# Routing operations handed out four at a time late in the attention, and the first second-layer weights' differences moved from VectorE to GpSimd

## The chip, the cores and the metric

The kernel runs on one core of a Trainium2 chip. The metric is the device time of one execution in microseconds. Three runs of the kernel before gave 551.42, 549.42 and 554.98 us, with a median of 551.42 us.

## What is computed

A block attention feeds a mixture of experts. The attention has 4 batches, 8 heads, 768 positions and head size 64. Each query sees a window of its neighbours (distance under 16) and 24 block summaries (maximum of the keys and mean of the values over 32 positions). Its output, 3072 tokens of 512 numbers, goes through a two-level router:

```
g_idx = argmax(x @ w_group);  e_idx = argmax(x @ w_expert[g_idx])
h = relu(x @ w1[g, e]);  out = (g_w * e_w) * (h @ w2[g, e])
```

There are 4 groups of 4 experts, so 16 experts, each with a 512x1024 and a 1024x512 matrix. One token goes to one expert. Everything is float32; the expert products are made from a rounded part and the difference to it (three matmuls for one product).

## The kernel before

**Attention.** `attention` (L591) runs 48 steps and three more that drain the pipeline (L905). A step scores a third of a head pair (`scores`), takes exponentials on ScalarE (`exps`), transposes them on TensorE and copies them out on ScalarE (`transpose_p`), multiplies by the values (`values`, whose results VectorE divides by the row sums into `xt`), and works on the next head pair (`prep`: copies `kf` and `kw`, block maxima `ks`) and on the router's logits (`logits`: transposes of `xt`, the copy `xT`, and the matmul into `ps_lg`). Each engine takes its work in the order in which it is written; the order is made by hand, and no scheduler changes it.

**Routing inside the attention.** For three of the four batches the router's work is handed out in between. `Router.route` and `Router.ranks` turn logits into expert, rank inside the expert and weight, some 27 small VectorE operations a batch (maxima `mx`, differences `dd`, one-hots `c` and `eoh`, casts `sb` and `eb`, then seven small ranking matmuls on TensorE, then `rk`, `sums`, `rf`, `ri`, the one-hot rows `ohr`, and the weights `we`, `wf`, `w_all`). They are generators that stop after each operation, and they are added to a list after steps 16, 28 and 40. The second one is followed by `first_blocks`, which finds the largest expert and makes the tables `t_first_gather`, `t_first_weight` and `t_first_scatter` of its first four blocks of 128 tokens. `advance` (L597) takes operations off the list: one behind `scores`, one behind the reciprocal of `values`, one behind its multiplication, two in `prep` part 4 (`OPS`, L61). It stops early at a pause. In the attention `clock.pe` is minus infinity, so a pause before a matmul always lasts until the next step. What is left when the steps are over is written out in one piece (L962).

**The hook.** Late steps also start the experts (`hook`, L1350): the difference of the first expert's first weights is made in four parts behind steps 44 to 47 (`split_w`: ScalarE rounds `w1h`, VectorE subtracts to `w1l`), the tokens are gathered by GpSimd behind steps 44 and 47, and the first blocks of matmuls of `first` are written behind steps 49 to 51.

**First expert blocks.** `first` (L1261) handles two pairs of 128-token blocks. `stage1_2` makes the hidden layer in eight groups of 12 matmuls (k = 0 to 7), with a rounding `hTh` on ScalarE and a difference `hTl` on VectorE after every second group; `stage2` makes the outputs, 24 matmuls a block. In the first pair, groups k = 4 to 7 each write one quarter of the second weights' rounding `w2h` on ScalarE and of their difference `w2l` on VectorE (L1264).

**Routing behind the attention.** The fourth batch's routing, the tables of all units (`units`, `unit_rows`, `unit_slots`) and their matmuls `ps_lg<-bo_unit` form one generator, `fin`. The main loop (L1403) hands its operations out after each group of matmuls by the planner's own count: `clock.pe` grows by an estimate for each matmul (107 for a 256-column one, 213 for a 512-column one), `clock.dve` by 85 plus the columns for each VectorE instruction, and operations are handed out while `clock.dve` is below `clock.pe`. A pause waits until `clock.pe` is 300 (ranking) or 800 (table matmuls) ahead. What is left when `first` reports "units" is written in one piece. Then the pairs of all experts follow (`pair`, L1147).

Of the kernel before, what the change touches and what calls it, by code (L numbers as in the profile page):

```python
# [58 lines left out]

ROUTE_AT = (16, 28, 40)  # L60
OPS = dict(r=1, m=1, k=2, s=(1, 1, 1))  # L61


W1_AT = 34
# [10 lines left out]
class Banks:  # L75
# [5 lines left out]
    def next(self):  # L81
        self.n += 1
        return self.tiles[(self.n - 1) % len(self.tiles)]
# [6 lines left out]
class Clock:  # L90

    pe, dve = float("-inf"), 0.0
    step = 0


def columns(ap):
# [494 lines left out]
def attention(tc, q, k, v, w_group, w_expert, ident, x_dram, ps, router, hook):  # L591
# [3 lines left out]
    clock = router.clock  # L595

    def advance(ops):  # L597

        for _ in range(ops):
            r = next(work[0], work) if work else "wait"  # L600
            if r is work:
                work.pop(0)
            elif r == "wait":
                break

    def need(bit):

        while not router.ready & bit:
            clock.step += 1
            advance(99)  # L610
# [5 lines left out]
    with ExitStack() as st, ExitStack() as nat_st:  # L616
# [54 lines left out]
        def init_va(i):  # L671
            va = va_ring[i]
            V.memset(va[0:PAD, 0], 0.0)
            V.memset(va[64:KW, NQT - 1], 0.0)

            nc.gpsimd.memset(va[96:NR, :, :, 0:D], 0.0)
            V.memset(va[96:NR, :, :, D:D + 1], EPS)
            V.memset(va[0:NC, :, :, D:D + 1], 1.0)
# [40 lines left out]
        def block_sums(idx):  # L719

            sp = ps_tr.next()[:, 0:2 * D]
            va = va_ring[idx % NVA]
            for i in range(NQT // 4):
                for j in range(4):
                    T.matmul(out=sp[32 * j:32 * j + 32], lhsT=pick[:, i], rhs=va[0:KW, NQT // 4 * j + i, :, 0:D],
                             start=(i == 0), stop=(i == NQT // 4 - 1), skip_group_check=True)
            vss[idx] = sm.tile([P, 2 * D], F32, name="vs", bufs=2)
            V.tensor_copy(out=vss[idx], in_=sp)
# [8 lines left out]
        def put_vs(idx):  # L737
            vs = vss.pop(idx)
            vr = wk.tile([NC, 1, 2, D], F32, name="vr")
            n = NBLK // 4  # L740
            for j in range(4):
                nc.sync.dma_start(out=vr[KW + n * j:KW + n * j + n, 0].rearrange("p h d -> p (h d)"), in_=vs[32 * j:32 * j + n])
            vrs[idx] = vr
# [10 lines left out]
        def copy_1port(out, src):  # L754

            V.tensor_reduce(out=out, in_=src.unsqueeze(src.ndim), axis=AX.X, op=ALU.max)

        def prep(idx, part):
# [27 lines left out]
            else:  # L786
# [5 lines left out]
                             in_=kf[:, PAD:PAD + S].rearrange("p (a k) -> p a k", k=BLOCK))  # L792
                advance(OPS["k"])
                copy_1port(kw[:, :, KW:NC], ks[:, None, :].broadcast_to([P, NQT, NBLK]))

        def scores(n):

            idx, g = n // 3, n % 3
            qt, kw = qts[idx % 2], kws[idx % 2]
            sp = [ps_s.next()[:, 0:2 * NC].rearrange("p (j c) -> p j c", j=2) for _ in range(2)]  # L800
            for j in range(2):
                for i, h in ((0, 0), (1, 1), (1, 0), (0, 1)):
                    t, rows = 4 * g + 2 * j + i, slice(64 * h, 64 * h + 64)
                    T.matmul(out=sp[h][64 * i:64 * i + 64, j], lhsT=qt[rows, QT * t:QT * t + QT],
                             rhs=kw[rows, t], start=True, stop=True, skip_group_check=True)
            nm = sm.tile([P, 4], F32, name="nm")
            ss = sm.tile([P, 4, NC], F32, name="ss", bufs=2)
            for h in range(2):
                for j in range(2):
                    u, t = 2 * h + j, 4 * g + 2 * j  # L810
                    V.tensor_tensor_reduce(out=ss[:, u], in0=mask[:, 1 if t == 0 else 2 if t == NQT - 2 else 0],  # L811
                                           in1=sp[h][:, j], scale=1.0, scalar=3.4e38, op0=ALU.add, op1=ALU.min,
                                           accum_out=nm[:, u:u + 1])
            advance(OPS["s"][g])
            return ss, nm

        def exps(n, sp, nm):
            pr = prr[n % 3]
            for i in range(4):
                nc.scalar.activation(out=pr[:, i, 0:NC], in_=sp[:, i], func=AF.Exp, bias=nm[:, i:i + 1], scale=-1.0)  # L820
            return pr

        def transpose_p(pr):
            pt = ps_tr.next()
            for i in range(4):
                T.transpose(out=pt[0:NR, i * P:(i + 1) * P], in_=pr[:, i], identity=ident)
            ptS = wk.tile([NR, 4, P], F32, name="ptS", bufs=3)
            nc.scalar.copy(out=ptS.rearrange("p a c -> p (a c)"), in_=pt[0:NR])  # L828
            return ptS

        def values(idx, g, ptS):
# [3 lines left out]
            for u in range(4):  # L835
                h, j = u // 2, u % 2
                for i in range(2):
# [4 lines left out]
            V.reciprocal(out=rs, in_=av[:, :, :, D:D + 1])  # L842
            advance(OPS["r"])
            V.tensor_tensor(out=x[:, 2 * g:2 * g + 2, 2 * a * D:2 * (a + 1) * D].rearrange("p j (h d) -> p j h d", h=2),
                            in0=av[:, :, :, 0:D], in1=rs.broadcast_to([P, 2, 2, D]), op=ALU.mult)
            advance(OPS["m"])

# [57 lines left out]

        for n in range(NG + 3):
            idx, g = n // 3, n % 3
            if n < NG:
                b, a = order[idx]
                xs[b] = x_ring[b % 2]  # L910
            for step in PLAN[g]:
                if step == "s" and n < NG:
                    sps = scores(n)
                    if n == 0:
                        block_sums(0)
                        put_vs(0)
                        router.consts()
                elif step == "e" and n < NG:
                    prs[n] = exps(n, *sps)
                elif step == "t" and 0 <= n - T_LAG < NG:  # L920
                    pts[n - T_LAG] = transpose_p(prs.pop(n - T_LAG))
                elif step == "v" and 0 <= n - V_LAG < NG:
                    values((n - V_LAG) // 3, (n - V_LAG) % 3, pts.pop(n - V_LAG))
                elif step[0] == "p" and n < NG and idx + 1 < len(order):
                    prep(idx + 1, int(step[1]))
                elif step == "b" and n < NG and idx + 1 < len(order):
                    block_sums(idx + 1)
                elif step[0] == "l" and 0 <= idx - LAG[step] < len(order):
                    logits(idx - LAG[step], int(step[1]))
            if n == 0:  # L930
                init_va(2)
                spread_vs(0)
                init_va(3)
            if n in ROUTE_AT:
                b1 = ROUTE_AT.index(n)
                work.append(router.route(b1 * TB, (b1 + 1) * TB))
                if b1 == 1:
                    work.append(router.first_blocks())
            if n == NG - 4:
                nat_st.close()  # L940
            if n < NG:
                if g == 0 and 0 < idx < len(order) - 3:
                    qk[idx + 3] = load_qk(idx + 3)
                if g == 0 and idx + 2 < len(order):
                    load_vw(idx + 2)
                if g == 2 and idx + 1 < len(order):
                    put_vs(idx + 1)
                if g == 0 and idx > 0:
                    spread_vs(idx)
            if g == 1 and stores:  # L950
                store()
            while stores and n == NG - 5:
                store()
            clock.step += 1
            hook(n, need, w1_space)
# [11 lines left out]
class Experts:  # L967
# [293 lines left out]
    def first(self):  # L1261
        for i in range(0, NE, 2):
            for k, _ in enumerate(self.stage1_2(0)):
                if i == 0 and k >= 4:  # L1264
                    self.split_w(("first", 0), 1, [k - 4])
                yield
            if i + 2 < NE:
                self.x_t1()
                yield
            for half in range(2):  # L1270
                s2 = self.stage2([t[:, :, half * P:half * P + P] for t in self.hT2], ("first", i + half))
                if i + half < NE - 1:
                    yield from s2
        yield "units"
        for part, _ in enumerate(s2):
            self.split_w(("unit", 0), 0, [part])
            if part == 0:
                self.x_t2(0)
                for i in range(2):
                    self.gather_one(i)  # L1280
                self.gather_small(0)
        self.fixed = True
# [153 lines left out]
```

## Time and profile before

| | before |
|---|---|
| median of three runs | 551.42 us |
| the profiled execution | 553.0 us |
| its span | 551.3 us |
| mean granted TensorE clock | 0.953 of 2.4 GHz |
| TensorE busy | 496.8 us (90%) |
| VectorE busy | 312.7 us (57%) |
| ScalarE busy | 288.9 us (52%) |
| GpSimd busy | 152.9 us (28%) |

The span runs from the first to the last instruction; the execution's own time is 1.7 us longer. The attention lasts until about 200 us of the span, the first expert's blocks until about 258 us, and the other units follow. In rows of a timeline the first number is the start and the second the length in us; in brackets stands the idle time of the engine just before and what ended it. PE is TensorE, DVE VectorE, ACT ScalarE, POOL GpSimd, SPq the queue of SyncE's transfers. L122 is the helper that records every operation of the router and the experts, so those rows are told apart by their tiles.

### The profile page before, as it was taken

To read this page: it belongs to the slowest core of one execution; us is meant where nothing else is said; L and a number is where in the kernel's file an instruction comes from. 1 tells how busy PE (TensorE), PEld (TensorE's weight loads), DVE (VectorE), ACT (ScalarE), POOL (GpSimd) and SP (SyncE) were. 2 spreads that over 40 slices of the span, in tenths; PEclk is the share of its full clock that TensorE was granted. 3 is DMA by queue.
4 is the path that set the end of the run, shared out by engine and by line. 5 is a ranking of instruction groups with operands and counts; after the bars stand their busy time and mean duration, and the time that the engine had idled before them with its cause. 6 is when DMAs were issued, how large, how long until landed. Compare 5 with 4: busy or idle time off the path is not lost. (4 is left out here: it accounts for less than half of the span.)

```text
span 551.3 us, 13196 instructions
## 1 busy us (share of the span) xinstructions
PE 496.8 (90%) x4873; PEld 416.4 (76%) x4873; DVE 312.7 (57%) x1001; ACT 288.9 (52%) x561; POOL 152.9 (28%) x166
## 2 busy tenths in 40 slices
PE   7798888898988688989979999999999999999990
PEld 4576666676767577978959798889898998977760
DVE  6767778788866558866715445365474745630000
ACT  4788867899967433215615444455463644631110
POOL 6553533353444100045122040402021230211110
PEclk8899979999988799997999999999999999999996
DMA  9676855795671610099918969667656667637930
GB/s 212 148 186 152 204 143 140 165 213 146 142 269 40 248 59 21 19 352 394 365 37 314 356 251 393 235 211 272 214 203 224 210 213 248 212 121 251 340 117 27
DMA packets 80840, 111.18 MB, mean 202 GB/s; under 512 B 42732, under 2 KB 51310, under 8 KB 77936
## 3 DMA queue, kind: packets, MB, share of 16 engines
q1 hardware_dynamic: 74992, 93.31, 54.3%
q0 software_dynamic: 4704, 14.69, 7.1%
q10 hardware_dynamic: 1056, 2.10, 1.1%
q8 instruction: 45, 0.74, 0.6%
q14 instruction: 43, 0.35, 0.2%
HBM read 122.46 MB, written 13.04 MB: 246 GB/s over the span
## 5 line engine op out<-in xcount | busy, mean ns | idle before, releaser
L122 PE MATMUL ps_s<-xT,w1h 128*128 128x256 f32 x448 | 85.1, 287 | 1.9 <-DVE hTl L122 1.5
L122 DVE TENSOR_TENSOR w2l<-w2r,w2h 128x1024 fp32r<-128x1024 f32 x40 | 48.8, 1225 | 54.4 <-ACT w2h L1061 52.6
L1105 POOL DMA_INDIRECT out_dram<-y,t_unit_scatter x21 | 23.8, 1134 | 197.4 <-ACT y L1099 112.7
L122 PEld LDWEIGHTS ps_s<-xT,w1h 128*128 128x128 f32 x448 | 71.5, 193 | 3.4 <-DVE hTl L122 1.7
L122 PE MATMUL ps_s<-xT,w1l 128*128 128x256 f32 x224 | 63.7, 285 | 0.0
L820 ACT ACTIVATE pr<-ss,nm 128x120 f32<-128x120 f32 x192 | 60.1, 388 | 3.6 <-DVE nm L811 3.2
L1143 ACT ACTIVATE hTh<-ps_s 128x512 fp32r<-128x512 f32 x44 | 26.3, 598 | 54.1 <-PE ps_s L122 34.1
L749 POOL TENSOR_TENSOR va<-vr,share 24x512 f32<-24x512 f32 x48 | 49.7, 1060 | 11.7 <-DMA vr<-vs 8.3
L122 DVE TENSOR_TENSOR w1l<-w1r,w1h 128x1024 fp32r<-128x1024 f32 x40 | 46.4, 1221 | 2.9 <-ACT w1h L1061 2.9
L122 PE MATMUL ps_s<-ohr,w1h 128*128 128x256 f32 x256 | 48.1, 286 | 0.0
L122 DVE SCALAR_TENSOR_TENSOR hTl<-ps_s,hTh 128x512 fp32r<-128x512 f32 x44 | 30.4, 691 | 25.6 <-ACT hTh L1143 25.4
L811 DVE CUSTOM_DVE_ANT_0 ss<-mask,ps_s 128x120 f32<-128x120 f32 x192 | 42.0, 273 | 4.1 <-ACT pr L820 2.5
L1061 ACT CAST w2h<-w2r 128x1024 fp32r<-128x1024 f32 x40 | 41.5, 1042 | 4.3 <-DVE w_all L122 3.6
L122 PEld LDWEIGHTS ps_s<-xT,w1l 128*128 128x128 f32 x224 | 43.2, 193 | 0.2
L122 PEld LDWEIGHTS ps_s<-ohr,w1h 128*128 128x128 f32 x256 | 40.5, 192 | 0.7 <-issue 0.6
L828 ACT COPY ptS<-ps_tr 121x512 f32<-121x512 f32 x48 | 28.1, 586 | 21.8 <-PE ps_tr L122 8.7
L1061 ACT CAST w1h<-w1r 128x1024 fp32r<-128x1024 f32 x40 | 38.9, 1047 | 0.0
L789 POOL COPY kw<-kf 128x1152 f32<-128x1152 f32 x15 | 17.4, 1157 | 77.3 <-DVE kf L780 43.3
L122 PE MATMUL ps_s<-kw,qt 64*64 64x120 f32 x768 | 34.4, 290 | 4.4 <-DVE nm L811 2.3
L776 ACT ACTIVATE qt<-ps_tr 64x384 f32<-64x384 f32 x64 | 33.4, 522 | 5.9 <-PE ps_tr L122 4.9
L122 PE MATMUL ps_s<-ohr,w1l 128*128 128x256 f32 x128 | 36.3, 284 | 0.0
L122 PE MATMUL ps_av<-va,ptS 121*64 121x65 f32 x768 | 34.3, 234 | 2.0 <-DVE mx L122 1.3
(255 smaller groups left out, 1058.5 us busy)
## 6 DMA issues: line engine op xcount, KB each, us to landing
w1r<-in_moe_w_dram SPq DMA_DIRECT2D x42, 1024.0 KB
w2r<-in_moe_w_dram SPq DMA_DIRECT2D x42, 1024.0 KB
va<-in_v_dram SPq DMA_DIRECT2D x32, 240.0 KB
kn<-in_k_dram SPq DMA_DIRECT2D x16, 384.0 KB
qn<-in_q_dram SPq DMA_DIRECT2D x16, 384.0 KB
x_dram<-xt SPq DMA_DIRECT2D x12, 512.0 KB
w_first<-in_moe_w_dram SPq DMA_DIRECT2D x2, 1024.0 KB
w2r<-in_moe_w_dram ACTq DMA_DIRECT2D x2, 1024.0 KB
```

Of the source, the lines that this page charges most:

```text
L122: return f(*args, **kw)
L749: nc.gpsimd.tensor_tensor(out=va_ring[idx % NVA][KW:NC, t:t + n, :, 0:D], in0=vr[KW:NC].broadcast_to([NBLK, n, 2, D]), in1=by(share, KW, N ...
L776: nc.scalar.activation(out=by_run(qb, h)[:, j], in_=tv, func=AF.Copy, scale=-1.0 / 8.0)
L789: (nc.gpsimd if idx else V).tensor_copy(out=kw[:, :, 0:KW], in_=tiles)
L811: V.tensor_tensor_reduce(out=ss[:, u], in0=mask[:, 1 if t == 0 else 2 if t == NQT - 2 else 0], in1=sp[h][:, j], scale=1.0, scalar=3.4e38, ...
L820: nc.scalar.activation(out=pr[:, i, 0:NC], in_=sp[:, i], func=AF.Exp, bias=nm[:, i:i + 1], scale=-1.0)
L828: nc.scalar.copy(out=ptS.rearrange("p a c -> p (a c)"), in_=pt[0:NR])
L1061: (copy or self.nc.scalar.copy)(out=h, in_=src)
L1105: self.nc.gpsimd.indirect_dma_start(out=out, out_offset=bass.IndirectOffsetOnAxis(ap=self.tabs[name, "scatter"][:, col:col + 1], axis=0), ...
L1143: nc.scalar.activation(out=th[:, js], in_=hp, func=AF.Relu)
```

## The change

From step 41 on, every call of `advance` may take four times as many operations. The four subtractions that make `w2l` for the first expert are issued to GpSimd instead of VectorE. GpSimd's instructions are not counted in `clock.dve`.

```diff
 OPS = dict(r=1, m=1, k=2, s=(1, 1, 1))
+MORE_AT, MORE = 41, 4
...
 class Clock:
...
-    step = 0
+    step, n = 0, 0
...
     def advance(ops):
-        for _ in range(ops):
+        for _ in range(ops * (MORE if clock.n >= MORE_AT else 1)):
...
         for n in range(NG + 3):
             idx, g = n // 3, n % 3
+            clock.n = n
...
             for k, _ in enumerate(self.stage1_2(0)):
                 if i == 0 and k >= 4:
-                    self.split_w(("first", 0), 1, [k - 4])
+                    self.split_w(("first", 0), 1, [k - 4], sub=self.nc.gpsimd)
                 yield
```

## Rows read from the trace of the kernel before

**Rows 1.** The page's 40 equal slices of the span (13.8 us each): busy tenths of TensorE, VectorE and GpSimd, and the granted clock in tenths.

```profile
PE   7798888898988688989979999999999999999990
DVE  6767778788866558866715445365474745630000
POOL 6553533353444100045122040402021230211110
PEclk8899979999988799997999999999999999999996
```

**Rows 2.** Stretches of the span: us, then busy time of PE, PEld, DVE, ACT and POOL with instruction counts, granted clock, DMA share, GB/s. The last row is another answer of the same view, for PE alone.

```profile
150.00:160.00 10.00, 8.37 (x155) 6.70 (x155) 9.09 (x50) 9.82 (x27) 4.61 (x5) 1.00 0.77 251
...
245.00:250.00 5.00, 3.93 (x18) 3.15 (x18) 3.46 (x14) 0.00 (x0) 3.44 (x4) 0.72 1.02 388
250.00:255.00 5.00, 5.00 (x19) 4.20 (x18) 2.14 (x4) 2.50 (x4) 3.29 (x3) 0.60 1.03 418
...
200.06:257.58 57.52, 52.59 (x323) 0.94 0.42 160
```

**Rows 3.** TensorE's timeline from step 42 to the first pair of units: the rows with waits, and the rows around them.

```profile
160.43 1.47 PE L122 MATMUL ps_tr<-bo_first,ohr 128*128 128x4 f32 x12 [1.33 <-DVE bo_first L122]
...
200.30 0.36 PE L122 MATMUL ps_s<-xT,w1h 128*128 128x256 f32 x1
...
203.14 0.28 PE L122 MATMUL ps_s<-xT,w1h 128*128 128x256 f32 x1
204.87 0.39 PE L122 MATMUL ps_s<-xT,w1h 128*128 128x256 f32 x1 [1.45 <-DVE hTl L122]
...
214.81 0.20 PE L122 MATMUL ps_tr<-eb,tri 128*128 128x96 bf16 x1 [1.64 <-DVE eb L122]
...
244.11 1.35 PE L122 MATMUL ps_lg<-bo_unit,ohr 128*128 128x132 f32 x8 [0.42 <-issue]
...
247.86 0.63 PE L122 MATMUL ps_lg<-few,copies 32*128 32x32 f32 x2 [0.86 <-DVE t_unit_scatter L122]
```

**Rows 4.** VectorE's timeline at the end of the attention: the first and the last operation of what is left of the third batch's routing (17 instructions), two rows inside it, and the next `hTl`; then ScalarE's rows beside them.

```profile
200.48 0.26 DVE L122 TENSOR_TENSOR rk<-eoh,ps_tr 128x96 f32<-128x96 f32 x1 [0.84 <-PE ps_tr L122]
...
203.21 0.18 DVE L122 TENSOR_TENSOR we<-sums,c 128x24 f32<-128x24 f32 x1
...
204.05 0.17 DVE L122 TENSOR_TENSOR w_all<-wf,w_all 128x6 fp32r<-128x6 f32 x1
204.13 0.68 DVE L122 SCALAR_TENSOR_TENSOR hTl<-ps_s,hTh 128x512 fp32r<-128x512 f32 x1
205.53 1.23 DVE L122 TENSOR_TENSOR w2l<-w2r,w2h 128x1024 fp32r<-128x1024 f32 x1 [0.71 <-ACT w2h L1061]
...
200.26 0.60 ACT L1143 ACTIVATE hTh<-ps_s 128x512 fp32r<-128x512 f32 x1 [1.28 <-PE ps_s L122]
204.45 2.00 ACT L1061 CAST w2h<-w2r 128x1024 fp32r<-128x1024 f32 x2 [3.59 <-DVE w_all L122]
```

**Rows 5.** Steps 45 and 46 of the attention on VectorE, ScalarE, GpSimd and TensorE.

```profile
173.65 0.16 DVE L122 COPY sc_first<-ps_tr 128x8 f32<-128x8 f32 x1
...
174.35 0.42 DVE L865 COPY xT<-ps_tr 128x256 f32<-128x256 f32 x1
175.45 1.40 DVE L122 TENSOR_TENSOR w1l<-w_first,w1h 128x1024 fp32r<-128x1024 f32 x1 [0.69 <-ACT w1h L1061]
...
177.14 1.25 ACT L820 ACTIVATE pr<-ss,nm 128x120 f32<-128x120 f32 x4 [0.22 <-DVE nm L811]
...
174.72 4.03 POOL L749 TENSOR_TENSOR va<-vr,share 24x512 f32<-24x512 f32 x3 [2.51 <-issue]
...
174.82 0.53 PE L122 MATMUL ps_lg<-xT,wcat 128*32 128x192 f32 x8 [0.79 <-DVE xT L865]
```

**Rows 6.** VectorE's small operations beside GpSimd's multiplications: three GpSimd instructions, two VectorE operations that fall into them, and the spread (least, median, most, in ns) of such operations over the four batches.

```profile
120.81 3.04 POOL L749 TENSOR_TENSOR va<-vr,share 24x512 f32<-24x512 f32 x3
...
122.05 0.86 DVE L122 CAST eb<-eoh 128x96 bf16<-128x96 f32 x1
123.12 0.76 DVE L122 TENSOR_TENSOR seen<-seen,cs 128x16 f32<-128x16 f32 x1
...
L122 DVE CAST eb<-eoh x4: 194/200/860, 79.7 to 214.6; 128x96 bf16<-128x96 f32 x4
L122 DVE TENSOR_REDUCE cs<-eoh x4: 291/306/314, 78.3 to 214.3; 128x16 f32<-128x96 f32 x4
```

**Rows 7.** Groups of instructions over the whole span: busy us and mean ns of one, then idle time before them.

```profile
L749 POOL TENSOR_TENSOR va<-vr,share 24x512 f32<-24x512 f32 x48 | 49.7, 1060 | 11.7 <-DMA vr<-vs 8.3 <-issue 2.5
L789 POOL COPY kw<-kf 128x1152 f32<-128x1152 f32 x15 | 17.4, 1157 | 77.3 <-DVE kf L780 43.3 <-ACT kf L780 22.1 <-DVE xT L865 6.3
```

**Rows 8.** The fourth batch's routing on VectorE, from its first operation to the cast that the ranking matmuls need (nine instructions).

```profile
212.47 0.27 DVE L122 TENSOR_REDUCE mx<-lg 128x30 f32<-128x120 f32 x1
...
214.21 0.17 DVE L122 CAST sb<-seen 128x16 bf16<-128x16 f32 x1
...
214.56 0.20 DVE L122 CAST eb<-eoh 128x96 bf16<-128x96 f32 x1
```

**Rows 9.** The clock after TensorE waits, in stretches of 1 us (columns as in rows 2).

```profile
186.00:187.00 1.00, 0.00 (x0) 0.00 (x0) 1.00 (x5) 0.00 (x0) 0.00 (x0) 0.50 1.08 414
...
191.00:192.00 1.00, 1.00 (x7) 1.00 (x7) 0.48 (x3) 0.00 (x0) 0.00 (x0) 0.50 0.00 0
```

## The prediction

> **What bounds the kernel now.** I began with the slices: TensorE is at 9 tenths or more almost everywhere behind the attention, and lower only before slice 16 and in slice 18 [rows 1]. So the part behind 200 us is worth what TensorE waits there, and anything that starts it later costs in full. Next I took TensorE's own timeline. From 200.06 us, where the fourth group of expert matmuls ends, to 257.58, where the first pair of units begins, it has 57.52 us, of which 52.59 busy at a mean clock of 0.94 [rows 2]. The waits are few: 1.45 us for `hTl`, 1.64 us for `eb`, and some around the table matmuls from 244 to 248 us [rows 3], after which the clock was 0.72 and 0.60 [rows 2]. So 57.52 - 52.59 = 4.9 us are waits. A mean of 0.94 with levels 1.0 and 0.5 means 12% of 57.5 us at 1.2 GHz, half of which, 3.4 us, is lost. Together 8.3 us can be had here. Then I looked at what the waits hang on. `hTl` stands behind 17 left-over routing instructions, 200.48 to 204.13 us, and ScalarE's `w2h` waited 3.59 us for the last of them [rows 4]. Inside the attention I read steps 45 and 46: VectorE waits for ScalarE's `w1h`, ScalarE's exponentials wait for VectorE's scores, and TensorE for `xT` [rows 5]. There a delay on VectorE goes round this chain to the end.
>
> **Part one, four operations a place.** Counted by the code: step 41 takes seven operations to the end of the first table's first product, then meets a pause; step 42 takes three; step 43 finishes `first_blocks` and does eight operations of the third batch; step 44 does two and the exponential; step 45 does twelve (`rk` to the reciprocal); step 46 the last five. Nothing is left behind the attention.
>
> Steps 41 to 44: TensorE's 1.33 us wait for `bo_first` [rows 3] moves up a step. VectorE was busy 9.09 of 10 us there [rows 2], so `bo_first` comes late there too: I take the same wait, so 0. The bounds are -1.3 (no wait) and +1.3 (twice the wait, since now two table products stand ahead of step 44 in place of one).
>
> Step 45: in the trace 1.8 us lie between `sc_first` (173.65) and `w1l` (175.45), with 0.69 of them idle [rows 5]. The twelve operations from `rk` to the reciprocal, 200.48 to 203.21, take 2.7 us [rows 4]. They replace about 0.25 us of small ones and the idle, so `w1l` is 2.7 - 0.25 - 0.69 = 1.75 us later, and with it the scores of step 46, its exponentials and the chain behind. GpSimd's three multiplications of this step also lie there [rows 5], and they can hold VectorE up (below) by some 1.75 us more. I take +2.2, less 0.2 for two operations that leave step 48: **+2.0** (1.5 to 3.3). ScalarE's exponential `dd` moves into step 44, under 0.35 us, inside the same bounds. Step 46's five lie in an idle stretch before the next `w1l`. The gathers on GpSimd's queue and the stores on SyncE's queue keep their places.
>
> The left-over batch: gone, with TensorE's 1.45 us wait and ScalarE's 3.59 us [rows 3, 4].
>
> **Part two, GpSimd subtracts.** VectorE is rid of four instructions. The planner no longer counts 4 x (85 + 1024) for it, so it hands out the fourth batch sooner. By its count: after group k = 4 `clock.pe` is 1284 and `clock.dve` 597, so `mx`, `dd`, `c`, `mx` go out; after k = 5 (2568) come `c`, `eoh`, `sb`, `cs`, `eb`, `seen` and one cast; after k = 6 (3852) come the ranking matmuls. Before, they came behind 18 matmuls of `stage2`. All later table work moves up by 5120, one block of `stage2`, so nothing is left to write in one piece at 244 us. **That saves the 8.3 us** above, the 1.45 included (at least 4.9, if the clock falls all the same), less 0.4 us of new small waits where table products follow each other (0 to 1).
>
> What is late next: the ranking matmuls wait for `eb`, and all of TensorE's later work waits behind them. Now `eb` shares its time with GpSimd's subtractions. While GpSimd multiplies, VectorE's `eb` took 0.86 us and `seen` 0.76, each until about the end of a GpSimd instruction (120.81 + 2 x 1.01 = 122.84, and 123.85), where medians are near 0.2; the reduction `cs` never stretched [rows 6]. So an operation with two operands in memory, or a cast, waits for the end of the GpSimd instruction in hand, and GpSimd's next begins right behind it. Between `mx` and `eb` such operations are `dd`, `c`, `c`, `eoh`, `sb` and `eb`.
>
> The price of a subtraction is not in the trace. GpSimd's two-operand instruction takes 1060 ns for 512 columns, its copy 1157 ns for 1152 [rows 7]: 1.0 to 2.07 ns a column, 1.05 to 2.1 us for 1024. The two-operand row is the nearest, on fewer partitions; **I take 2.1 us**.
>
> The page GPSIMD Engine Reference of the Trainium skill (section 3.1, elementwise cycle accounting) speaks against such a move: it gives 4497 ns for a two-input float32 addition of 2048 columns, about twice VectorE's. Half of that, an estimate of 2.25 us, would make my sum 0.6 us dearer.
>
> The wait: `hTh` begins at 200.26; `w2h` can follow 0.5 us later, and the difference began 1.08 us behind `w2h` [rows 4], so GpSimd subtracts from 201.8 on and ends at 210.2. `hTl` ends near 201.5, and `dd` slips in just ahead. `c` then waits to 203.9, the second `c` to 206.0, `eoh` to 208.1, `sb` to 210.2, and 0.55 us later `eb` is done [rows 8]: 210.8. TensorE, with 24 matmuls in 2.9 us [rows 3], has finished k = 4 to 6 by 204.4. **It waits 6.4 us.** Were `dd` caught by the first subtraction, ScalarE's `dd` and `hTh` and so the third `w2h` would slip, GpSimd would pause, and `eb` would be done at 207.9: 3.5 us. The waits of VectorE's `hTl` and `rk` in this stretch lie beside TensorE's.
>
> Behind such a wait the clock falls: TensorE did nothing from 186 to 187 us, and the clock was 0.50 from there to 192, with TensorE busy at the end of it [rows 9]. That lost half of about 5 us. I take **+1.6** (0 to 2.6).
>
> **Sum**: 0 + 2.0 - 8.3 + 0.4 + 6.4 + 1.6 = **+2.1 us**. The profiled execution took 553.0 us with a span of 551.3, 1.6 us above the median; so 555.1 on its scale and **553.5 us** on the median's.
>
> **The rivals.** *GpSimd doesn't hold VectorE up here.* The subtractions fall between its operations, or cost 1 us each and wait for `w2h`. Then `eb` is done before TensorE asks, and 6.4 and 1.6 fall away: -5.9 us, 545.5 us. For it: ScalarE delivers a `w2h` only every 1.0 us, and VectorE comes in at each boundary. Against: both stretched rows [rows 6]. 13%.
>
> *GpSimd is slower.* Place: the same wait. Each 0.1 us on a subtraction costs 0.4. From 2.95 us each the sum passes +5.5 us; at 3.2 us it is +6.5, 557.9 us. For it: the row that I scale has 24 partitions, and VectorE's operations can also delay GpSimd (three multiplications took 4.03 beside `w1l`, not 3.04 [rows 5, 6]). Against: the copy on 128 partitions shows no such cost. 17%, with step 45 at its upper bound included.
>
> *The short wait* (`dd` caught): -0.8 us, 550.6 us. 15%.
>
> *The places don't give fourfold*: pauses stop them, and a rest is still left behind step 51. Then step 45's cost goes and the 1.45 us wait stays: +1.5 us. The count speaks against it. 5%.
>
> **How the numbers follow.** The forecast gets 50%. The runs before spread over 1% (549.42 to 554.98), so about 1%, 5.5 us, is what the measurement can tell. Forecast, short wait and missing fourfold lie within it, 70%; the first rival gives most of faster, 13%; the second slower, 17%. The range takes in all but the ends of the two rivals: 546 to 558.5.
>
> **What would show it.** No routing rows of the third batch behind 200 us, and `w2h` right behind `hTh` (part one); four GpSimd rows `w2l` of about 2.1 us, with VectorE's `c`, `eoh`, `sb` stretched to their ends; a TensorE wait for `eb` of 3.5 to 6.4 us ahead of the last group of the first hidden layer and a stretch at 0.5 behind it; no rest of table matmuls in one piece, and no cold stretch before the first pair; `w1l` of step 45 1.75 to 3.5 us later in its step. The prediction is wrong if `eb` is ready before TensorE asks, if GpSimd's subtraction is far from 2.1 us, or if the chain of steps 45 to 48 has slack that I don't see.

## The result: 0.9% slower, and where the time went

The changed kernel took 555.82 us as the median of its runs, the kernel before 550.94 beside it: a ratio of 1.0089, 95% interval 1.0068 to 1.0109, so +4.9 us (3.7 to 6.0). The forecast was 553.5 us (+2.1), a change within 1%, with a range of 546 to 558.5; both held, and the size came out about twice as large. The profiled execution took 554.71 us, of which 553.0 are its span.

The stage times below count from the first operation of step 41, `of` (152.16 us after, 155.04 before). The instructions ahead of it are the same in both kernels, yet that part was 2.9 us shorter in the profile of after, so only differences from `of` on are read.

| stage (us) | before | after |
|---|---|---|
| `of` to the first expert matmul `ps_s<-xT,w1h` (190.53, 191.08) | 35.49 | 38.92 |
| from there to the first pair of units (257.58, 259.11) | 67.05 | 68.03 |
| from there to the end of the span | 293.72 | 293.89 |

So 3.4 us were lost inside the attention, in steps 41 to 48, and 1.0 us behind it: +4.6 in this profile, beside +4.9 of the medians. One profile doesn't fix the first of these: the five kernels below that take the same steps of the attention lose 2.2 to 4.2 us there.

First the slices of the kernel after, TensorE and its clock, to be laid beside [rows 1].

```profile
PE   7898989889986776999989999899999999999990
...
PEclk8899999999987797999999999999999999999995
```

The sixteenth digit (207 to 221 us) is 6 where it was 8 (an 8 that the prediction passes over in [rows 1]), with the clock at 7: a new hole. Slice 19, where the clock was 7 before, is at 9. Next the stretches, with PE's busy time, the clock, the DMA share and GB/s; first all from the end of the fourth group of expert matmuls to the first pair, then the hole.

```profile
200.53:259.11 58.58, 50.57 (x315) 0.94 0.48 179
...
209.00:210.00 1.00, 0.00 (x0) 0.95 0.00 0
210.00:211.00 1.00, 0.00 (x0) 0.50 0.00 0
...
215.00:216.00 1.00, 1.00 (x7) 0.50 0.00 0
216.00:217.00 1.00, 1.00 (x8) 0.64 0.00 0
```

TensorE waits 58.58 - 50.57 = 8.0 us in this stretch, 4.9 before [rows 2]. The clock falls during the wait, which costs nothing, and stays at 0.50 from 212.18, where TensorE starts again, to about 216.7, which does: half of the 3.8 us up to 216 and 0.36 us of the next one, 2.3 us lost. The cold stretch ahead of the first pair [rows 2] is gone; here all engines and the clock:

```profile
245.00:250.00 5.00, 4.98 (x27) 3.97 (x27) 2.71 (x10) 0.00 (x0) 2.00 (x2) 1.00 1.03 410
250.00:255.00 5.00, 5.00 (x27) 4.23 (x26) 1.03 (x5) 1.97 (x3) 1.02 (x1) 1.00 1.03 390
```

What TensorE waits for, in its timeline, from step 42 to the ranking matmuls (compare [rows 3]):

```profile
153.94 1.52 PE L123 MATMUL ps_tr<-bo_first,ohr 128*128 128x4 f32 x12 [1.31 <-DVE bo_first L123]
...
175.75 0.87 PE L123 MATMUL ps_lg<-xT,wcat 128*32 128x192 f32 x8 [3.82 <-DVE xT L866]
...
212.18 0.26 PE L123 MATMUL ps_tr<-eb,tri 128*128 128x96 bf16 x1 [7.24 <-DVE eb L123]
```

The wait for `bo_first` is the old one, a step earlier. The second, for step 45's `xT`, is 3.82 us where it was 0.79: the delay of that step, seen from TensorE. The 7.24 us wait for `eb` is the hole. The 1.45 us wait for `hTl` is gone. Now VectorE and GpSimd ahead of that `eb`:

```profile
202.29 9.47 POOL L1064 TENSOR_TENSOR w2l<-w2r,w2h 128x1024 fp32r<-128x1024 f32 x4 [17.30 <-ACT w2h L1063]
...
202.21 0.28 DVE L123 TENSOR_TENSOR dd<-lg,mx 128x120 f32<-128x120 f32 x1
202.53 2.38 DVE L123 SCALAR_TENSOR_TENSOR c<-dd,iom 128x120 f32<-128x120 f32 x1
204.94 0.28 DVE L123 TENSOR_REDUCE mx<-c 128x30 f32<-128x120 f32 x1
205.25 2.00 DVE L123 TENSOR_TENSOR c<-iom,mx 128x120 f32<-128x120 f32 x1
207.28 2.28 DVE L123 TENSOR_TENSOR eoh<-c 128x96 f32<-128x96 f32 x1
209.49 2.30 DVE L123 CAST sb<-seen 128x16 bf16<-128x16 f32 x1
211.71 0.30 DVE L123 TENSOR_REDUCE cs<-eoh 128x16 f32<-128x96 f32 x1
211.93 0.19 DVE L123 CAST eb<-eoh 128x96 bf16<-128x96 f32 x1
```

This is the staircase of the forecast. GpSimd's four subtractions take 9.47 us, 2.37 each, one right behind the other. Four of VectorE's operations, which take 0.17 to 0.28 us by themselves [rows 8], take 2.0 to 2.4: each begins inside one GpSimd instruction, ends with it, and the next is caught by the next. `dd` slipped in ahead, by 0.08 us (202.21 against 202.29). The reduction `mx` lies beside the second subtraction and is not stretched; `cs` begins only as the last one ends.

Last, step 45 (compare [rows 5]):

```profile
171.56 0.24 DVE L123 TENSOR_TENSOR rk<-eoh,ps_tr 128x96 f32<-128x96 f32 x1
...
173.29 1.87 DVE L123 TENSOR_TENSOR ohr<-io,rf 128x384 fp32r<-128x384 f32 x2
...
175.61 1.53 DVE L123 TENSOR_TENSOR w1l<-w_first,w1h 128x1024 fp32r<-128x1024 f32 x1
...
173.27 4.77 POOL L750 TENSOR_TENSOR va<-vr,share 24x512 f32<-24x512 f32 x3 [2.69 <-issue]
```

The routing operations stand ahead of `w1l`, without the idle time that was there, and the pair `ohr` takes 1.87 us beside GpSimd's multiplications (1.02 elsewhere, in the part-two experiment below). From `w1l` of step 44 to that of step 45 there are 6.04 us, 3.74 before.

### The profile page after: what moved, and what is told of

It is laid out like the page before. It is cut to its first block, busy times and chain, and to the rows that moved or that the text cites. A ratio compares the mean times of both kernels' runs of the same rounds, so it can differ in the third digit from the quotient of the medians.

```text
span 553.0 us, 13196 instructions
## 1 busy us (share of the span) xinstructions
PE 492.7 (89%) x4873; PEld 413.9 (75%) x4873; DVE 316.5 (57%) x997; ACT 289.4 (52%) x561; POOL 159.5 (29%) x170
## 5 line engine op out<-in xcount | busy, mean ns | idle before, releaser
L123 PE MATMUL ps_s<-xT,w1h 128*128 128x256 f32 x448 | 86.7, 290 | 0.4 <-PEq L1318 0.4
L123 DVE TENSOR_TENSOR w2l<-w2r,w2h 128x1024 fp32r<-128x1024 f32 x36 | 44.1, 1225 | 54.1 <-ACT w2h L1063 53.8
L123 PE MATMUL ps_av<-w2h,hTh 128*128 128x512 f32 x88 | 35.1, 399 | 0.0
```

What stands on the lines that cost most here:

```text
L123: return f(*args, **kw)
```

## The experiments

Each kernel was timed beside the kernel before, which the ratio is to. It is not the quotient of two medians, from which it differs by up to 0.24 points; differences in us between kernels are worked out from it. The table gives the profile's stages of each, in us: 1 from `of` to the first expert matmul, 2 from there to the first pair, 3 from there to the end; then TensorE's wait for `eb`.

| kernel | ratio, 95% interval | stage 1 | stage 2 | stage 3 | wait for `eb` |
|---|---|---|---|---|---|
| before | 1 | 35.49 | 67.05 | 293.72 | 1.64 |
| after | 1.0089 (1.0068 to 1.0109) | 38.92 | 68.03 | 293.89 | 7.24 |
| part one alone | 1.0002 (0.9970 to 1.0033) | 37.73 | 63.16 | 293.72 | about 0 |
| part two alone | 1.0116 (1.0088 to 1.0143) | 35.57 | 73.88 | 292.15 | 8.50 |
| both, GpSimd's time counted | 1.0047 (1.0017 to 1.0076) | 39.72 | 63.89 | 293.70 | 1.87 |
| both, VectorE subtracts uncounted | 0.9957 (0.9927 to 0.9986) | 37.81 | 61.93 | 291.79 | 1.79 |
| after, fourfold from step 48 | 1.0030 (1.0003 to 1.0057) | 36.49 | 68.97 | 292.39 | 7.23 |
| part one, from step 48 | 0.9973 (0.9942 to 1.0004) | 36.55 | 63.71 | 293.77 | about 0 |
| VectorE uncounted, from step 48 | 0.9909 (0.9872 to 0.9945) | 36.45 | 61.59 | 292.20 | 1.79 |
| after, subtractions in halves | 1.0000 (0.9968 to 1.0032) | 39.56 | 65.37 | 292.93 | 3.85 |

**Part one alone.** VectorE subtracts and is counted for it, as before.

```diff
-                    self.split_w(("first", 0), 1, [k - 4], sub=self.nc.gpsimd)
+                    self.split_w(("first", 0), 1, [k - 4])
```

> Part one alone: four operations a place from step 41, the subtractions back on VectorE and counted as before. Theory (the time is lost in two places: step 45's twelve operations make the attention end about 3 us later, and the ranking matmuls wait 7 us for eb because GpSimd's subtractions hold VectorE up): step 45 stays dear, TensorE's wait of 1.45 us for hTl is gone, the wait for eb falls from 7.2 us to under 1, and the table matmuls at the end are written in one piece again with a cold stretch behind them. Sum against the kernel before: +3 - 1.45 - 1.6 = 0, within -1 to +1.5 us. Rival (the attention's end is only later by chance, the routing operations cost nothing there): -3 us.

The time stayed the same: 550.58 us. Stage 1 is 2.2 us longer, stage 2 is 3.9 shorter: the left-over routing is gone from behind the attention, and its price is paid in front of it. The profile's net gain of 1.7 us does not show in the medians, whose interval reaches from -1.7 to +1.8. In this profile GpSimd's multiplications hold the pair `ohr` of step 45 longer than in the kernel after (1.87 us):

```profile
172.76 2.74 DVE L123 TENSOR_TENSOR ohr<-io,rf 128x384 fp32r<-128x384 f32 x2
```

**Part two alone.** The places give single operations, as before.

```diff
-MORE_AT, MORE = 41, 4
+MORE_AT, MORE = 41, 1
```

> Part two alone: the subtractions on GpSimd, one operation a place as before. Theory: the third batch's rest stays behind the attention, hTl's wait of 1.45 us stays, the attention ends as early as before; GpSimd starts to subtract near 205.6 us, VectorE's operations stretch to the ends of the subtractions, and the ranking matmuls wait 6 to 7 us for eb with about 2 us at the lower clock behind it; against that the waits at eb and at the table matmuls and the cold stretch of before go, 6.9 us. Sum +1 to +3 us against before. Rival (only step 45 costs, GpSimd's part gains): -5 us.

It was much slower than I expected, +6.4 us. Here TensorE and VectorE:

```profile
202.91 0.39 PE L123 MATMUL ps_s<-xT,w1h 128*128 128x256 f32 x1 [1.46 <-DVE hTl L123]
...
213.11 0.24 PE L123 MATMUL ps_tr<-eb,tri 128*128 128x96 bf16 x1 [8.50 <-issue]
...
204.02 2.11 DVE L123 TENSOR_TENSOR c<-iom,mx 128x120 f32<-128x120 f32 x1
206.16 2.28 DVE L123 TENSOR_TENSOR eoh<-c 128x96 f32<-128x96 f32 x1
208.37 2.30 DVE L123 CAST sb<-seen 128x16 bf16<-128x16 f32 x1
210.59 0.30 DVE L123 TENSOR_REDUCE cs<-eoh 128x16 f32<-128x96 f32 x1
210.81 2.20 DVE L123 CAST eb<-eoh 128x96 bf16<-128x96 f32 x1
```

The left-over routing keeps its place, so the wait for `hTl` stays, and the subtractions begin later against the fourth batch: at 203.62, 1.0 us before TensorE has to wait for `eb`, where the kernel after has 2.65 us. The first `c` comes through, and the last subtraction then catches `eb` instead: again four are stretched, now `c`, `eoh`, `sb` and `eb`. The profile names no releaser for the 8.50 us ("issue"), but `eb` ends at 213.01, just ahead of the matmul. I had not followed which operation the last subtraction would meet.

**Both, with GpSimd's time counted.** The planner adds the subtractions to VectorE's clock although GpSimd does them, so the fourth batch is handed out at its old places.

```diff
+    def count(self, *args, **kw):
+        self.router.clock.dve += vector_ns(VECTOR_NS, *args, **kw)
...
-                    self.split_w(("first", 0), 1, [k - 4], sub=self.nc.gpsimd)
+                    self.split_w(("first", 0), 1, [k - 4], sub=Timed(self.nc.gpsimd, self.count))
```

> Both parts, but the planner counts GpSimd's four subtractions in VectorE's time as before, so the ranking and table matmuls go back to their old places. Theory: the fourth batch's routing comes behind the subtractions or beside the last of them, so the wait for eb is 1 to 2 us in place of 7.2, while the cold stretch before the first pair comes back; step 45 stays dear. Sum against before: +3 - 1.45 = +1 to +2.5 us. Rival (GpSimd's subtractions cost wherever the ranking stands, since TensorE needs their result): +4 us or more.

It came out at 553.16 us, +2.6. GpSimd's four rows are about as long as in the kernel after (9.55 us), but only one VectorE operation of the chain, the first `c`, is held to the end of one:

```profile
202.92 9.55 POOL L123 TENSOR_TENSOR w2l<-w2r,w2h 128x1024 fp32r<-128x1024 f32 x4 [17.31 <-ACT w2h L1063]
...
210.25 2.35 DVE L123 SCALAR_TENSOR_TENSOR c<-dd,iom 128x120 f32<-128x120 f32 x1
...
214.05 0.20 PE L123 MATMUL ps_tr<-eb,tri 128*128 128x96 bf16 x1 [1.87 <-DVE eb L123]
```

So the long wait needs both: GpSimd's subtractions, and a fourth batch that is handed out among them.

**Both, VectorE subtracts, uncounted.** The order of TensorE's instructions is that of the kernel after; only the engine that subtracts is the old one.

```diff
-                    self.split_w(("first", 0), 1, [k - 4], sub=self.nc.gpsimd)
+                    self.split_w(("first", 0), 1, [k - 4], sub=self.nc.vector)
```

> Both parts, but VectorE makes the four subtractions, still uncounted: TensorE's order is that of the changed kernel, instruction for instruction. Theory: nothing holds VectorE up but its own subtractions, so eb is done 1.5 to 3 us after TensorE asks instead of 7.2 us, the clock stays up, and the cold stretch before the first pair stays away: the changed kernel's time less 5 to 7 us, that is -2 to 0 us against before, with step 45 still costing 3. Rival (the early place of the ranking matmuls itself is what costs, whoever subtracts): as the changed kernel, +4 to +5 us.

It took 547.99 us, -2.4, and is 1.0089 - 0.9957 = 1.3% or 7.3 us faster than the kernel after. In the profile stage 2, where the subtractions lie, is 68.03 - 61.93 = 6.1 us shorter. Another 1.1 us lie in stage 1, ahead of any subtraction, and 2.1 us in stage 3, where the clock differs (last section), so not all of the difference between the two profiles is GpSimd's. The next pair is cleaner: from step 48 on the same exchange is worth 6.7 us by the ratios, and stages 1 and 3 agree within 0.2 us. The earlier places of the fourth batch look like a gain by themselves: with VectorE subtracting in both, they are worth 2.5 us here against part one alone, and 3.5 us from step 48 on. The intervals overlap a little in both pairs, and in the profiles only 1.2 and 2.1 us lie in stage 2, with most of the rest in stage 3, so the size is not fixed. VectorE had the time for the four subtractions all along.

**The fourfold from step 48 on**, with GpSimd's subtractions, with VectorE's counted ones, and with VectorE's uncounted ones: the line below alone, then with each of the edits of `split_w` shown above.

```diff
-MORE_AT, MORE = 41, 4
+MORE_AT, MORE = 48, 4
```

> The changed kernel with the fourfold places from step 48 on, where VectorE idles 3 to 4 us a step, in place of step 41. Theory (step 45's twelve operations delay the chain of w1l, scores and exponentials by 2.3 to 3 us): w1l of step 45 comes 3.7 us after that of step 44 again, not 6.0, one routing operation at most is left behind the attention, and the wait for eb stays 7 to 8 us. The changed kernel's time less 2.5 to 3 us: +2 us against before. Rival (the attention's end is set elsewhere, by the clock or the loads): no change from the changed kernel, +5 us.

> Part one alone with the fourfold places from step 48. Theory: step 45 costs nothing, the rest behind the attention is gone with its wait of 1.45 us, and the wait for eb of 1.64 goes too: -2.5 to -3 us against before. Rival (the rest behind the attention was hidden, so part one gains nothing wherever it stands): 0.

> Fourfold places from step 48, the four subtractions on VectorE and uncounted. Theory: the gain of the uncounted order (2.4 us against before with step 45 dear) and the 2.5 us of step 45 add up: -4.5 to -5.5 us against before, wait for eb near 1.8 us, no cold stretch before the first pair. Rival (the two share a slack): -2.5 us, as with step 41.

They took 553.19 (+1.7), 549.89 (-1.5) and 546.38 us (-5.0). The -1.5 is not clear of noise: its interval takes in both 0, the rival, and the -2.5 to -3 that I expected. By the ratios each is faster than its twin that starts at step 41, by 3.2, 1.6 and 2.6 us; only the first of these three is well clear of noise. The lengths of stage 1 agree with them: it is 36.5 us in all three, only 1.0 above the kernel before where the twins have 2.2 to 3.4; some of the routing now lies behind the first expert matmul, and stage 2 stands 0.3 below to 0.9 above that of the twins. In the first of them step 45 has its old length and the wait for `eb` its new one:

```profile
169.20 1.23 DVE L123 TENSOR_TENSOR w1l<-w_first,w1h 128x1024 fp32r<-128x1024 f32 x1 [2.10 <-ACT w1h L1063]
...
172.94 1.75 DVE L123 TENSOR_TENSOR w1l<-w_first,w1h 128x1024 fp32r<-128x1024 f32 x1 [0.68 <-ACT w1h L1063]
...
211.65 0.26 PE L123 MATMUL ps_tr<-eb,tri 128*128 128x96 bf16 x1 [7.23 <-DVE eb L123]
```

From `w1l` to `w1l` 3.74 us, as before, with the 0.68 us of idle time back. The two prices are separate: one is removed here and the other stays whole. Not all of its gain over the kernel after is from there, though: 1.5 us in the profile lie in stage 3 (last section). The third kernel, with neither price, beats both:

```profile
201.07 1.23 DVE L1064 TENSOR_TENSOR w2l<-w2r,w2h 128x1024 fp32r<-128x1024 f32 x1 [0.24 <-ACT w2h L1063]
...
203.35 1.21 DVE L1064 TENSOR_TENSOR w2l<-w2r,w2h 128x1024 fp32r<-128x1024 f32 x1
204.48 0.28 DVE L123 TENSOR_TENSOR c<-iom,mx 128x120 f32<-128x120 f32 x1
...
205.32 0.20 DVE L123 CAST eb<-eoh 128x96 bf16<-128x96 f32 x1
...
205.58 0.22 PE L123 MATMUL ps_tr<-eb,tri 128*128 128x96 bf16 x1 [1.79 <-DVE eb L123]
```

Two subtractions of 1.2 us stand among the routing operations, none of these is stretched, and `eb` is done at 205.5 in place of 212.1 us.

**Halves.** The kernel after, with each of GpSimd's subtractions cut into two of 512 columns. If a VectorE operation waits for the end of the GpSimd instruction in hand, shorter instructions shorten each wait; if the two share a bandwidth, the same columns cost the same.

```diff
-            (sub or self.V).tensor_tensor(out=l, in0=src, in1=h.bitcast(F32), op=ALU.subtract)
+            if sub:
+                for i in range(2):
+                    sub.tensor_tensor(out=l[:, i], in0=src[:, i], in1=h[:, i].bitcast(F32), op=ALU.subtract)
...
```

> The changed kernel with each of GpSimd's four subtractions cut into two of 512 columns. Theory (an operation of VectorE with two operands in memory, or a cast, waits for the end of the GpSimd instruction in hand and gets in there): the instructions take about 1.2 us each, each blocked operation waits up to 1.2 us in place of 2.3, eb is done some 3 to 4 us earlier, TensorE's wait for eb falls from 7.2 to 3 to 4.5 us: the changed kernel's time less 3 to 4 us, +1 to +2 us against before. Rival (the two engines share the memory's bandwidth, so VectorE is slowed for as long as GpSimd works at all): wait and time unchanged, +5 us.

It took 552.55 us, as long as the kernel before, so 4.9 us less than the kernel after by the ratios. The profile shows 2.7 us of that in stage 2 and 1.0 us in stage 3; its stage 1 is 0.6 us longer.

```profile
205.32 10.10 POOL L1066 TENSOR_TENSOR w2l<-w2r,w2h 128x512 fp32r<-128x512 f32 x8 [15.62 <-ACT w2h L1063]
...
205.56 1.26 DVE L123 SCALAR_TENSOR_TENSOR c<-dd,iom 128x120 f32<-128x120 f32 x1
...
207.17 0.95 DVE L123 TENSOR_TENSOR c<-iom,mx 128x120 f32<-128x120 f32 x1
208.16 1.21 DVE L123 TENSOR_TENSOR eoh<-c 128x96 f32<-128x96 f32 x1
...
210.66 1.12 DVE L123 CAST eb<-eoh 128x96 bf16<-128x96 f32 x1
...
214.13 0.68 DVE L123 SCALAR_TENSOR_TENSOR hTl<-ps_s,hTh 128x512 fp32r<-128x512 f32 x1
214.73 0.24 DVE L123 TENSOR_TENSOR rk<-eoh,ps_tr 128x96 f32<-128x96 f32 x1
...
211.83 0.22 PE L123 MATMUL ps_tr<-eb,tri 128*128 128x96 bf16 x1 [3.85 <-DVE eb L123]
```

GpSimd is busy longer (10.10 us, 1.26 a piece), and yet VectorE's stretched operations take 0.95 to 1.26 us in place of 2.0 to 2.4, and TensorE's wait is 3.85 us in place of 7.24. The wait goes with the length of the GpSimd instruction, not with its work. `hTl` and `rk`, whose second operand lies in PSUM, are not stretched beside GpSimd (214.13 and 214.73, while it works to 215.42).

## Why the prediction was right, and where its sizes were off

- **Nothing left behind the attention**: right. ScalarE's `w2h` begins at 201.16 right behind `hTh`, without the 3.59 us wait of [rows 4]:

```profile
200.67 0.60 ACT L1145 ACTIVATE hTh<-ps_s 128x512 fp32r<-128x512 f32 x1 [1.28 <-PE ps_s L123]
201.16 1.99 ACT L1063 CAST w2h<-w2r 128x1024 fp32r<-128x1024 f32 x2
```

- **Steps 41 to 44: 0 (bounds 1.3 either way).** From `of` to `w1l` of step 44 the kernel after takes 17.41 us, 16.67 before: +0.7. The five kernels with the fourfold from step 41 have 15.84 to 17.45, those without it 16.45 to 16.70, so even the sign of this term changes from profile to profile. The wait for `bo_first` moved up a step at its old size, as put.
- **Step 45: +2.0 (1.5 to 3.3), the first mis-sized term.** It measured +2.3 from `w1l` to `w1l` against the 2.2 that I took, and about 0.4 more up to the first expert matmul, where I had taken 0.2 off: +2.7. Both causes that were named are in the rows: the idle time is filled, and GpSimd's multiplications stretch `ohr`. This profile flatters the term: in the four other kernels with the same steps, the distance from `w1l` to `w1l` is 6.82 to 6.92 us, +3.1 to +3.2, and TensorE's wait for `xT` 4.6 to 4.7. There VectorE is held up by 0.8 to 0.9 us more while they run: `ohr` takes 2.74 us (part one alone, above), or the one-operand `sums` ahead of it 0.95 where it takes 0.17 in the kernel after (both parts, VectorE uncounted; 1.05 in the halves):

```profile
172.17 0.95 DVE L123 TENSOR_SCALAR sums<-sums 128x30 f32<-128x30 f32 x1
```

  So the 1.75 us that the forecast set aside for GpSimd's multiplications, and of which it took about a quarter, was mostly needed. Stage 1 as a whole is +3.4 with the 0.7 of steps 41 to 44. The later start shows that this was a cost of the place, not of the operations: from step 48 on stage 1 is only 1.0 longer.
- **The wait for `eb`: 6.4 us forecast, 7.24 measured.** `dd` slipped in, the four operations named were the four stretched, TensorE stood still where the forecast put it. The size fell short because a subtraction took 2.37 us, not the 2.1 that I scaled from a multiplication on 24 partitions [rows 7]: 4 x 0.27 = 1.1 us later. Some 0.2 us of that were given back, as the forecast counted its 0.55 us to the end of `eb` from the start of `sb` in [rows 8]; from the end of `sb` the trace has 0.33. Half of the figure in the Trainium skill's GPSIMD Engine Reference (section 3.1), an estimate of 2.25 us, was nearer than my row, and still 5% below the trace.
- **Why VectorE stands still**: the forecast had it from two stretched rows. The halves and the uncounted VectorE kernel show it from both sides: shorter GpSimd instructions shorten the wait, and without any it is 1.8 us, nearly the old one. The page SBUF — State Buffer of the Trainium skill (section Who interferes with whom) states the same rule: an instruction of VectorE with two inputs in SBUF contends with a GpSimd instruction that reads SBUF, for a pair of ports that is locked and not shared out; copies and casts can contend too, and on Trainium2 a reduction never does. The trace agrees: 2.38 us for `c`, 2.30 for the cast `sb`, and beside a subtraction 0.28 for the reduction `mx` and 0.30 for `cs` (the latter in part two alone).
- **The cold clock behind the wait: +1.6 forecast, 2.3 measured**, inside its 0 to 2.6. That is half of the cold time. The same instructions at the higher clock give less: from the first matmul on `eb` to the first on `bo_unit`, the kernel after takes 24.45 us, and the two kernels with VectorE uncounted, whose clock is 1.00 there, 22.54 and 22.55, so 1.9 us by this.
- **What is removed: -8.3.** The cold stretch and the old waits are gone, and the small waits left are 8.0 - 7.2 = 0.8 us where I took 0.4. The 8.3 itself was 0.3 too much: some 0.6 us of the cold time before (247.2 to 247.86) lie inside a wait of TensorE and were counted as both. The third batch's seven ranking matmuls (200.06 to 200.30 before), which now stand inside the attention, are 0.2 us that the forecast left out; they are also most of the difference between 323 and 315 matmuls. These rows add up to -8.0 - 0.2 + 0.8 + 7.2 + 2.3 = +2.1, and the stretch from 200 us to the first pair is only 58.58 - 57.52 = 1.1 us longer. Of the 1.0 us between them, 0.4 would go with the 1.9 for the cold clock; I can't place the rest.
- **The rivals.** That GpSimd doesn't hold VectorE up (-5.9) is refuted; the uncounted VectorE kernels show what it would have been worth, 7.3 and 6.7 us by the ratios against their GpSimd twins. The slower GpSimd (from 2.95 us each) did not come true, but its direction did. The short wait didn't come, as `dd` was not caught. The places did give fourfold.
- **The expectation that failed** is that of part two alone: I moved the sum's own 6.4 us wait over to it, in another alignment, where it became 8.5 us behind a wait for `hTl` that stays. Four more missed their ranges by less than their intervals: part one from step 48 gained 1.5 us, not 2.5 to 3; the halves came to 0, not +1 to +2; VectorE uncounted came to -2.4, not -2 to 0; and with GpSimd's time counted it was +2.6, not +1 to +2.5.

In sum, behind the attention +0.1 was forecast and +1.0 came, inside it +2.0 was forecast and +3.4 came. Both misses go the same way. The mechanisms were the forecast ones, and the sizes came out small; that behind the attention the sum lies within 1 us of the measured time is partly luck: the wait, its cold clock and the small waits came out 1.9 us above the forecast in all, and the stretch only 0.9.

## What to carry to other kernels

Before work moves to GpSimd, count the VectorE operations that can be held up (here those with two SBUF inputs, casts, and in two profiles a one-operand `sums`) that will lie beside it in a chain that another engine waits for, and charge each with a whole GpSimd instruction; here four tiny operations cost some 7 us, to spare VectorE four subtractions of 1.2 us for which it had the time. If it must be GpSimd, cut its instructions short: in halves the wait fell from 7.24 to 3.85 us. And where a planner's count of an engine decides the order of work, try the count without the move: here that order, together with the fourfold places from step 48 on, is 5.0 us faster than the kernel before.

## What I had not expected

The same wait behind the first pairs is followed by a cold clock in some profiles and not in others. Around 287 us TensorE waits for `eq_unit`; here its timeline in the kernel after, and then in the one with GpSimd's subtractions and the fourfold from step 48:

```profile
287.62 0.44 PE L123 MATMUL ps_tr<-ident,eq_unit 128*128 128x128 f32 x2 [1.79 <-ACT eq_unit L1241]
288.58 3.51 PE L123 MATMUL ps_lg<-w2r,eq_unit 128*32 128x128 f32 x64 [0.52 <-DVE eq_unit L123]
```

```profile
286.83 0.44 PE L123 MATMUL ps_tr<-ident,eq_unit 128*128 128x128 f32 x2 [1.90 <-ACT eq_unit L1241]
287.79 1.96 PE L123 MATMUL ps_lg<-w2r,eq_unit 128*32 128x128 f32 x64 [0.52 <-DVE eq_unit L123]
```

The waits are alike (1.79 and 0.52 us, 1.90 and 0.52), but the 64 small matmuls behind them take 3.51 us in the first and 1.96 in the second; the mean clock from 260 to 300 us is 0.96 and 1.00. Stage 3 in the table falls apart in the same way: 293.7 to 293.9 us in five profiles, with 0.96, and 291.8 to 292.9 in the other five, with 1.00. The split follows the order of the routing nearly, but not quite: all four kernels that hand out the fourth batch at its old places are among the cold ones, and of the six that hand it out early only the kernel after is. Whether it belongs to a kernel or to a single execution was not tried; the executions of the kernel after differ in their mean clock, from 0.947 (559.0 us) to 0.969 (552.34 us). Stage 2 has such a case, too: with VectorE uncounted the clock is 0.62, 0.50, 0.50 and 0.67 in the four us from 229 us on, behind a wait of 0.25 us, while from step 48 on the same matmuls behind the same wait run at 1.00. So the 61.93 us of that kernel's stage 2 hold 1.7 us of cold clock.
